# Reordering the opening of a fused depthwise-conv and feed-forward kernel: conv by token halves, other splits of loads, and output slots ahead of the second group

## The chip, the cores and the metric

The kernel runs on one core of one Trainium2 chip. The metric is device time in microseconds (us); the time before is the median of three runs. The engines are named as in the profile: PE is TensorE, DVE is VectorE, ACT is ScalarE, POOL is GpSimd, SP is SyncE. The last two mostly issue DMAs here.

## The reference

```
def attn(x, weight):                     # x (8, 4096, 192) f32, weight (8 heads, 7 taps)
    w = softmax(weight, axis=-1)         # with + 1e-9 in the denominator
    x_pad = zeros of 6 tokens in front of each sequence, then x
    out[b, s, h, g] = sum_k w[h, k] * x_pad[b, s + k, h, g]      # 24 channels a head

def moe(x, w_in, w_out):                 # x (32768, 192), w_in (192, 2048), w_out (2048, 192)
    h = x @ w_in
    g = maximum(0.01 * h, h)
    return g @ w_out

reference = moe(attn(x, weight).reshape(32768, 192), w_in, w_out)
```

A causal depthwise convolution of 7 taps, a matrix product up to 2048 features, a leaky relu, and a matrix product back to 192.

## The kernel before

**Layout.** Channels stand on partitions: three chunks `c` of 64 channels, and two batches (`e` = 0, 1) on the two partition halves. `xt` holds the transposed input, `yt` the result of the conv, `g` the relu's output. A *block* is 512 tokens of a pair of batches; there are 32. Blocks 0 and 1 are cut into halves of 256 tokens, so the list `groups` has four groups of 256 (0 to 3) and then 30 of 512.

**Stages of a group.** (1) The conv makes `yt` from `xt`. On DVE it is `conv_jobs`: for each chunk, one multiplication (L222) and six multiply-adds (L228) with the taps in `wk`. On PE it is `pe_conv_jobs` (L259): a tap is a diagonal matrix `diag[c]`, in a high and a low part, so that a chunk takes 2 parts x 7 taps x 2 batches = 28 matmuls, accumulated in a PSUM tile `acc` and then scaled by `rsum` into `yt` (`evac`; straight at L271, crossed between the partition halves at L276). Straight and crossed jobs run side by side on the array. (2) `mm1` (L507) makes one unit `u`: 12 matmuls of 256 columns into one of two `ph` buffers in PSUM, then a Prelu on ACT (L515) writes `g` and frees the buffer. A group of 256 tokens has eight units (two feature chunks of 128 each). (3) `mm2` multiplies by `w_out`. For groups 0 to 3 it runs in row slots (`mm2_row_slot`, L525): a slot is two matmuls, for the two row halves of one feature chunk `fc` and a pair `p` of output tiles; round 0 and round 1 of a pair swap the halves, and between the rounds stands a *seal*, a small ACT instruction (or an output copy on ACT) that the first slot of the next round waits for. Later groups use the transposed form at L588, which this change leaves alone.

**The opening.** Only groups 0 and 1 have a conv on PE. Group 0: chunk 0 by its two parts in two accumulators (`hi`, and `low` through ACT, joined by DVE at L465), then chunks 1 and 2. Group 1: chunk 1 on DVE, chunks 0 and 2 on PE in three pieces, which `CUTS` puts behind the units 1, 3 and 5 of group 0. From group 2 on the conv is all DVE's, in the order `SKEW`, issued one group ahead.

Input: `x_half` 0 is loaded by SP and transposed on PE. `x_rows` 1 and 2 (groups 1 and 2) are loaded by POOL, transposed on PE (L167, `transpose_first`) into the PSUM tile `ptr`, and copied into `xt` by `evac_first` (L195). `x_half` 3 and all later blocks are loaded by POOL's DMAs and transposed by DMAs that SP issues. `w_in[0]` and `w_in[1]` are loaded by POOL; copies on DVE (`spread_up` L326, `spread_down` L322) put the rows also on the other partition half. `near` and `far` are the halves of the 1024 columns of one `w_in`.

**What sets the order.** The schedule is by hand: each engine runs its instructions in the order of the program text. POOL issues, in this order: `w_in` 0 in three DMAs with `x_rows` 1 between, `w_in` 1 in two, `x_rows` 2, `w_out` in two, then computes `wk` (L445, L446), then issues `x_half` 3 and block 2. `plan`, `quota` and `between` say how many mm2 row slots stand between and behind mm1's units in each step of two units; the slots of group i belong to the tiles of group i - 1.

PSUM: `ptr`, `acc` and `po` tiles share one ring of four buffers, so a new one waits until the oldest has been read.

Of the kernel before, what the change touches and what calls it, by code (L numbers as in the profile page):

```python
# [10 lines left out]
FP32 = mybir.dt.float32  # L11
BF16 = mybir.dt.bfloat16
# [3 lines left out]
def kernel(  # L16
# [33 lines left out]
    for k in range(K):  # L50
        SKEW += [(2, k), next(pair)]
    SKEW += [(1, 5), (0, 6), (1, 6)]
    CUTS = {1: (0, 6), 3: (6, 11), 5: (11, 14)}
    GB = 32
    NR = D // (2 * GB)

# [79 lines left out]

    def load_first(q):
        rows = x[0:2, q * HT : (q + 1) * HT, :].rearrange("e (s p) d -> p e s d", s=HS)
        if q == 0:
            x_nat[q] = stage_pool.tile([128, 2, HS, D], FP32, name="x_nat")  # L140
            for s in range(HS):
                nc.sync.dma_start(out=x_nat[q][:, :, s], in_=rows[:, :, s])
        elif q in x_rows:
            for e in range(2):
                nc.gpsimd.dma_start(out=x_rows[q][:, e], in_=rows[:, e])  # L145
        else:
            for c in range(NCH):
                for e in range(2):
                    nc.gpsimd.dma_start(  # L149
                        out=x_half[q][:, c, :, e, :],  # L150
                        in_=rows[:, e, :, c * CH : (c + 1) * CH],
                    )
# [9 lines left out]
    def transpose_first(q, mid=None):  # L162
        if q:
            t = psum_o.tile([128, HS, NCH, 128], BF16, name="ptr", tag="po")
            for s, c in product(range(HS), range(NCH)):
                for e in range(2):
                    nc.tensor.transpose(  # L167
                        out=t[e * CH : (e + 1) * CH, s, c, :],
                        in_=x_rows[q][:, e, s, c * CH : (c + 1) * CH],
                        identity=ident,  # L170
                    )
            ptr[q] = [t[:, s] for s in range(HS)]
            return
        ts = [
            psum_o.tile([128, NCH, 128], FP32, name=f"ptr{s}", tag="po") for s in range(HS)
        ]
        for s, t in enumerate(ts):
            if s and mid is not None:
                mid()
            for c in range(NCH):  # L180
                nc.tensor.matmul(
                    out=t[:, c, :],
                    lhsT=x_half[q][:, c, s, :, :].rearrange("p e k -> p (e k)"),
                    rhs=ident,
                    start=True,
                    stop=True,
                )
        ptr[q] = ts

    def evac_first(q, *copies):  # L190
        dst = xt[0][:, :, HALO + q * HT : HALO + (q + 1) * HT]
        dst = dst.rearrange("p c (s k) -> p s c k", s=HS)
        for s, t in enumerate(ptr.pop(q)):
            for cs in (slice(0, 1), slice(1, NCH)) if q == 0 and s else (slice(0, NCH),):
                copies[s](out=dst[:, s, cs], in_=t[:, cs])  # L195

    def transpose_half(q):
# [123 lines left out]
    def spread_down(n, copy=nc.vector.tensor_copy, cols=slice(0, WF)):  # L321
        copy(out=w_in[n][0:CH, 1, cols], in_=w_in[n][CH:128, 0, cols])  # L322
# [16 lines left out]
    load_w_in(0, 128, near)  # L339
    load_first(1)  # L340
    load_w_in(0, 128, far)
    for rows in (0, 128):
        load_w_in(1, rows)
    load_first(2)


    w_out = const_pool.tile([128, NFC, D], BF16)
    for h in range(2):
        cs = slice(h * NFC // (2 * RUN), (h + 1) * NFC // (2 * RUN))
        nc.gpsimd.dma_start(  # L350
            out=w_out.rearrange("p (c i) d -> p c i d", i=RUN)[:, cs],
            in_=moe_w_out.rearrange("(c p i) d -> p c i d", p=128, i=RUN)[:, cs],
        )


    wa = psum_h.tile([128, 2, ST], FP32, name="warm", tag="ph")
# [87 lines left out]
    wk = const_pool.tile([128, NCH, K], FP32, name="wk")  # L444
    nc.gpsimd.tensor_add(wk, taps[:, :, 0, 0:K, 0], wml[:, :, 0:K])  # L445
    nc.gpsimd.tensor_mul(wk, wk, rsum.to_broadcast([128, NCH, K]))  # L446
    load_first(3)
    load_x(2)
    diag_wide(1, 1)
    diag_wide(2, 1)  # L450
    spread_up(0, slice(0, 1), near)
    spread_down(0, cols=near)

    def act_scale(out, in_, scale):
        nc.scalar.activation(
            out=out, in_=in_, func=mybir.ActivationFunctionType.Copy, scale=scale
        )

    hi = acc_tile()
    low = const_pool.tile([128, HT], FP32, name="low")  # L460
    pe_hi, _ = pe_conv_jobs(groups[0], 0, parts=(0,), accs=[hi] * 2)
    pe_lo, evac_lo = pe_conv_jobs(groups[0], 0, cross=True, parts=(1,))
    run(pe_hi, pe_lo)
    evac_lo(act_scale, act_scale, out=low)
    nc.vector.scalar_tensor_tensor(  # L465
        out=y_of(groups[0], 0), in0=hi[:, :HT], scalar=rsum[:, 0, :], in1=low,
        op0=mybir.AluOpType.mult, op1=mybir.AluOpType.add,
    )
    spread_up(0, slice(2, 3), near)
    pe_1, evac_1 = pe_conv_jobs(groups[0], 1)  # L470
    pe_2, evac_2 = pe_conv_jobs(groups[0], 2, cross=True, accs=[acc_tile(), wps[:, 0]])
# [1 line left out]
    evac_1(act_scale)  # L473
    evac_2(nc.vector.tensor_scalar_mul, act_scale)
    spread_up(0, slice(0, 1), far)
    spread_down(0, nc.scalar.copy, far)


    g, po, acc2, osb, seal = {}, {}, {}, {}, None
# [8 lines left out]
    def mm1(grp, u, M):  # L488
# [9 lines left out]
        if wide:  # L498
            order = [(i, c) for c in chunks for i in range(nf)]
        for i, c in order:  # L500
            if wide and (i, c) == (0, 2):
                transpose_first(1)
            f = nf * u + i
            for e in range(2):
# [17 lines left out]
    def mm2_one(rt, m, fc, start, stop):  # L522
# [7 lines left out]
            stop=stop,  # L530
        )

    def mm2_row_slot(q):

        p, fc = divmod(q, 2 * NFC)
        rnd, fc = divmod(fc, NFC)
        pair = (2 * p, 2 * p + 1)
        first, last = fc == 0, fc == NFC - 1  # L540
# [112 lines left out]
        NSW - 1: [8, 8, 16, 16],  # L653
        NSW: [16, 8, 8, 16, 8, 8, 16, 16],
    }
    between = {(1, 0): (3, 5)}
    for i, js in ((NSW - 2, (2, 3)), (NSW - 1, (1, 2)), (NSW, (2, 3, 5, 6))):
        between.update({(i, j): (0, 4) for j in js})
    slot = 0
# [10 lines left out]
    for i, grp in enumerate(groups):  # L670
        blk, t0, T = grp
        steps = T // 64
        if t0 == 0:
            g[blk] = g_pool.tile([128, NFC, 2, ST], BF16, name="g", tag="g")
        quota = plan.get(i, [16] * 4 if T == HT else [5, 5, 6, 5, 5, 6, 8, 8])

        if i == 0:
            ahead = []
# [3 lines left out]
        for j in range(steps):  # L682
            early = between.get((i, j), (0, 0))
            for u in range(2 * j, 2 * j + 2):
                mm2_slots(i, early[u % 2])
                mm1(grp, u, 128 if i <= NSW else CH)
                if i == 0 and u == 0:
                    evac_first(1, nc.vector.tensor_copy, nc.vector.tensor_copy)
                    spread_up(0, slice(2, 3), far)
                    conv_1 = conv_jobs(groups[1], (1,))  # L690
                    run([conv_1[:3]])
                    spread_down(1)
                    spread_up(1, slice(0, 1), near)
                    spread_up(1, slice(2, 3))
                    run([conv_1[3:5]])
                    spread_up(1, slice(0, 1), far)
                    run([conv_1[5:]])
                    pe_0, evac_0 = pe_conv_jobs(groups[1], 0)
                    pe_2, evac_2 = pe_conv_jobs(groups[1], 2, cross=True)
                if i == 0 and u in CUTS:  # L700
                    cut = slice(*CUTS[u])
                    run(pe_0[cut], pe_2[cut])
                if i == 0 and u == 5:
                    evac_0(nc.vector.tensor_scalar_mul)
                    evac_2(nc.vector.tensor_scalar_mul, nc.vector.tensor_scalar_mul)
                if i == 0 and u == 6:
                    transpose_first(2)
                    evac_first(2, nc.vector.tensor_copy, nc.vector.tensor_copy)
            jobs = ahead[per * j : per * (j + 1)]
            if T == ST:  # L710

# [56 lines left out]
```

## Time and profile before

| what | value |
|---|---|
| median of the runs | 680.82 us (680.67 to 681.41, 3 runs) |
| span of the profiled execution | 679.2 us |
| PE busy | 674.9 us (99%) |
| ACT busy | 517.6 us (76%), 496.6 of it the Prelu L515 |
| DVE busy | 481.2 us (71%), 380.1 of it the conv L228 |
| POOL busy | 147.4 us (22%) |
| one Prelu (128x1024) | 1.02 us |
| first mm1 matmul | 8.09 us after the span's start |
| landing of `w_in[1]` | 12.19 and 12.77 us |
| landing of `x_rows` 2 | 13.28 and 13.81 us |
| landing of `w_out` | 15.73 and 17.59 us |

The span runs from the first to the last recorded instruction. A chain of waits lists what ended last, followed back from the end; its pieces are start, length, engine, tile and line, and how many instructions. In a timeline or a group line, `out<-in partitions x elements` says what an instruction reads and writes, and the bracket behind it the idle time of its engine just before and what ended that. Start-to-start spacings of single instructions are a little shorter than the durations, because an engine overlaps one's end with the next one's start.

### The profile page before, as it was taken

The numbers are of one execution on the slowest core, as the hardware profiler recorded it, in microseconds if no ns is written. First come the engines' busy times: TensorE is split into PE (matmuls) and PEld (weight loads), VectorE is DVE, ScalarE is ACT, GpSimd is POOL, SyncE is SP. The second block draws the span as 40 slices with busy tenths as digits, with TensorE's granted clock in tenths as the row PEclk, the third lists the DMA queues.
The fourth block names the chain that finished last, engine by engine and source line by source line (L and its number), as shares of the span: only waits on it lengthen the run. The fifth ranks groups of instructions, "written<-read, shape, count | busy, mean of one in ns | idle before, by whom it ended". The sixth has DMA issues, their size and how long they took to land.

```text
span 679.2 us, 27092 instructions
## 1 busy us (share of the span) xinstructions
PE 674.9 (99%) x12442; PEld 446.3 (66%) x12442; DVE 481.2 (71%) x816; ACT 517.6 (76%) x601; POOL 147.4 (22%) x208
## 2 busy tenths in 40 slices
PE   9999999999999999999999999999999999999998
PEld 6997666666666666666666666666666666666667
DVE  7989477866768766778667687667786676876612
ACT  7899877777787777777777777778777777777781
POOL 8455221122211222211222112222022220000000
PEclk9999999999999999999999999999999999999999
DMA  9999755655737656556556566567365573321123
GB/s 149 99 119 104 52 85 83 84 64 67 96 74 93 76 54 86 84 85 86 66 63 92 80 92 78 56 83 94 73 87 69 60 96 71 72 56 33 34 49 94
DMA packets 213970, 53.27 MB, mean 78 GB/s; under 512 B 209312, under 2 KB 213536, under 8 KB 213856
## 3 DMA queue, kind: packets, MB, share of 16 engines
q0 software_dynamic: 98832, 13.97, 30.3%
q1 hardware_dynamic: 115008, 37.57, 28.0%
q8 instruction: 97, 1.59, 0.9%
q14 instruction: 17, 0.14, 0.1%
q10 hardware_dynamic: 16, 0.00, 0.0%
HBM read 28.31 MB, written 25.17 MB: 79 GB/s over the span
## 4 chain that ended last, share of the span: by engine, by line
PE 98%; DVE 1%; ACT 0%; issue 0%; ACTq 0%
PE ph L507 49%; PE acc L588 44%; PE po L525 5%; PE acc L259 0%; DVE diag L420 0%; PE ptr L167 0%; ACT L366 0%; ACTq L288 0%; DVE w_in L322 0%; DVE yt L465 0%; DVE o_sb L638 0%; DVE x_half L155 0%; ACT w L372 0%; DVE w_in L326 0%; ACT junk L366 0%
## 5 line engine op out<-in xcount | busy, mean ns | idle before, releaser
L515 ACT ACTIVATE g<-ph 128x1024 bf16<-128x1024 f32 x512 | 496.6, 1021 | 139.8 <-PE ph L507 139.6
L228 DVE SCALAR_TENSOR_TENSOR yt<-xt,wk,yt 128x512 bf16<-128x512 bf16 (+1 forms) x582 | 380.1, 715 | 0.2
L507 PE MATMUL ph<-yt,w_in 64*64 64x512 bf16 (+2 forms) x6048 | 377.5, 369 | 0.3 <-DVE yt L465 0.3
L588 PE MATMUL acc<-g,w_out 64*64 64x512 bf16 x5568 | 339.9, 376 | 0.0
L507 PEld LDWEIGHTS <-w_in 64*64 64x64 bf16 (+1 forms) x6048 | 229.7, 131 | 103.4 <-issue 1.1
L588 PEld LDWEIGHTS <-w_out 64*64 64x64 bf16 x5568 | 178.2, 118 | 118.8
L96 POOL DMA_DIRECT2D x_bf<-in_x_dram x180 | 133.9, 774 | 407.6 <-DMA xt<-x_bf 405.6
L610 DVE STREAM_TRANSPOSE o_t<-acc 128x512 f32<-128x512 f32 x87 | 72.9, 875 | 182.2 <-PE acc L588 182.2
L525 PE MATMUL po<-w_out,g 64*128 64x192 bf16 (+1 forms) x640 | 36.8, 243 | 0.0
L525 PEld LDWEIGHTS <-g 64*128 64x128 bf16 (+1 forms) x640 | 32.6, 95 | 3.2 <-issue 0.4
L222 DVE TENSOR_SCALAR yt<-xt,wk 128x512 bf16<-128x512 bf16 (+1 forms) x97 | 28.8, 320 | 2.4 <-DMA xt<-x_bf 2.4
L598 ACT COPY junk<-junk 128x1 f32<-128x1 f32 x58 | 11.1, 191 | 4.1
L638 DVE COPY o_sb<-po 128x192 f32<-128x192 f32 x8 | 2.8, 356 | 6.8 <-PE po L525 3.9
L638 ACT COPY o_sb<-po 128x192 f32<-128x192 f32 x16 | 5.1, 323 | 0.3
L259 PE MATMUL acc<-xt,diag 64*64 64x256 bf16 x126 | 4.7, 272 | 0.1
L149 POOL DMA_DIRECT2D x_half<-in_x_dram x6 | 4.3, 732 | 0.9 <-DMA w_in<-in_moe_w_in_dram 0.9
L259 PEld LDWEIGHTS <-diag 64*64 64x64 bf16 x140 | 3.7, 106 | 1.0 <-issue 0.4
L360 PE MATMUL warm<-const-bfloat16-1.0 128*128 128x512 bf16 (+2 forms) x8 | 3.3, 577 | 0.8 <-PEq L752 0.8
L145 POOL DMA_DIRECT2D x_rows<-in_x_dram x4 | 2.9, 746 | 0.0
L316 POOL DMA_DIRECT2D w_in<-in_moe_w_in_dram x5 | 2.9, 593 | 0.0
L360 PEld LDWEIGHTS <-const-bfloat16-1.0 128*128 128x128 bf16 x10 | 1.2, 128 | 2.2 <-issue 2.2
L326 DVE COPY w_in<-w_in 64x512 bf16<-64x512 bf16 (+1 forms) x7 | 2.3, 337 | 0.2
(52 smaller groups left out, 25.9 us busy)
## 6 DMA issues: line engine op xcount, KB each, us to landing
out_dram<-o_t SPq DMA_DIRECT2D x112, 192.0 KB, 4.7
x_bf<-in_x_dram POOLq DMA_DIRECT2D x180, 64.0 KB, 3.1
out_dram<-o_sb SPq DMA_DIRECT2D x8, 192.0 KB, 2.8
xt<-x_bf SPq DMA_TRANSPOSE x90, 3.2
w_out<-in_moe_w_out_dram POOLq DMA_DIRECT2D x2, 384.0 KB, 8.3
out_dram<-o_t SPq DMA_DIRECT2D x8, 96.0 KB, 2.4
out_dram<-o_sb SPq DMA_DIRECT2D x8, 96.0 KB, 1.7
w_in<-in_moe_w_in_dram POOLq DMA_DIRECT2D x2, 256.0 KB, 5.5
```

Of the source, the lines that this page charges most:

```text
L96: ins = nc.gpsimd.dma_start(out=t[:, c, :, e, :], in_=src[2 * rp + e, :, :, c * CH : (c + 1) * CH],)
L222: lambda s=src, d=dst, c=c: nc.vector.tensor_scalar_mul(d, s, wk[:, c, 0:1])
L228: lambda s=src, d=dst, c=c, k=k: nc.vector.scalar_tensor_tensor(out=d, in0=s, scalar=wk[:, c, k : k + 1], in1=d, op0=mybir.AluOpType.mult, ...
L259: lambda k=k, p=p, a=a, ps=ps, to=to, acc=accs[e]: nc.tensor.matmul(out=acc[to, :T], lhsT=diag[c][ps, p, k, :], rhs=xt[0][ps, c, a : a + T ...
L360: nc.tensor.matmul(out=to[:, 0:cols], lhsT=ones[:, 0:128], rhs=ones[:, 0:cols], start=True, stop=True,)
L507: nc.tensor.matmul(out=ph[m : m + M, e, i * T : (i + 1) * T], lhsT=w_in_of(f, e, c, m, m + M), rhs=y[ps, c, t0 : t0 + T], start=(c == chun ...
L515: act = nc.scalar.activation(out=g[blk][:, nf * u : nf * (u + 1), :, t0 : t0 + T], in_=ph.rearrange("p e (i t) -> p i e t", i=nf), func=my ...
L525: return nc.tensor.matmul(out=po[m], lhsT=g[b][ps, fc, e, s * 128 : (s + 1) * 128], rhs=w_out[ps, fc, :], start=start, stop=stop,)
L588: ins = nc.tensor.matmul(out=acc2[gi, r][e * CH : (e + 1) * CH, 0:T], lhsT=w_out_of(ps, fc, r), rhs=g[b][ps, fc, e, t0 : t0 + T], start=fi ...
L598: seal = nc.scalar.copy(out=junk, in_=junk)
L610: nc.vector.transpose(out=osb[gi, 0][:, 0 : T // GB, :, r], in_=acc2.pop((gi, r))[:, 0:T].rearrange("p (j k) -> p j k", k=GB),)
L638: ins = copy(out=o_sb[:, n % 2, :], in_=po.pop(n))
```

## The change

1. Group 0's chunk 0: no parts in two accumulators any more. The conv is done by two halves of 128 tokens, both parts each (`pe_conv_halves`), and ACT alone writes `yt`. The join at L465 is gone; the spread of `w_in[0]`'s far half downwards goes from ACT to DVE, and two spreads move behind the conv in the text.
2. Group 1's conv: `CUTS` is gone. Chunk 0 alone runs on PE, by token halves, in one piece behind unit 4; chunks 1 and 2 are 14 jobs on DVE, the last four behind the evacuation of chunk 0.
3. `w_in[1]` is loaded in column halves, four DMAs for two, and spread in six copies.
4. `x_rows` holds tokens in pairs: partition p has tokens 2p and 2p + 1. The evacuation reads `ptr` with the token parity innermost, chunks 1 and 2 first and chunk 0 then. For `x_rows` 2 it goes from DVE to ACT.
5. `w_out`'s two DMAs are issued behind `wk`.
6. `x_rows` 1 is transposed after 4 matmuls of unit 0 instead of 8.
7. Row slots: the first 64 are taken in another order (`row_slots`), 16 of them run ahead of group 1's unit 0 and 4 between units 0 and 1, and the rest of group 1's are spread between the units.

```diff
-    CUTS = {1: (0, 6), 3: (6, 11), 5: (11, 14)}
...
     def load_first(q):
         rows = x[0:2, q * HT : (q + 1) * HT, :].rearrange("e (s p) d -> p e s d", s=HS)
+        if q in x_rows:
+            rows = x[0:2, q * HT : (q + 1) * HT, :].rearrange("e (p s) d -> p e s d", s=HS)
...
-            ptr[q] = [t[:, s] for s in range(HS)]
+            ptr[q] = t
             return
...
     def evac_first(q, *copies):
         dst = xt[0][:, :, HALO + q * HT : HALO + (q + 1) * HT]
+        if q:
+            dst = dst.rearrange("p c (k s) -> p c k s", s=HS)
+            t = ptr.pop(q).rearrange("p s c k -> p c k s")
+            for copy, cs in zip(copies, (slice(1, NCH), slice(0, 1))):
+                copy(out=dst[:, cs], in_=t[:, cs])
+            return
         dst = dst.rearrange("p c (s k) -> p s c k", s=HS)
         for s, t in enumerate(ptr.pop(q)):
-            for cs in (slice(0, 1), slice(1, NCH)) if q == 0 and s else (slice(0, NCH),):
+            for cs in (slice(0, 1), slice(1, NCH)) if s else (slice(0, NCH),):
                 copies[s](out=dst[:, s, cs], in_=t[:, cs])
...
-    for rows in (0, 128):
-        load_w_in(1, rows)
+    for cols in (near, far):
+        for rows in (0, 128):
+            load_w_in(1, rows, cols)
     load_first(2)
-    w_out = const_pool.tile([128, NFC, D], BF16)
-    for h in range(2):
...
     nc.gpsimd.tensor_mul(wk, wk, rsum.to_broadcast([128, NCH, K]))
+    w_out = const_pool.tile([128, NFC, D], BF16)
+    for h in range(2):
...
     load_first(3)
     load_x(2)
     diag_wide(1, 1)
     diag_wide(2, 1)
-    spread_up(0, slice(0, 1), near)
-    spread_down(0, cols=near)
...
-    hi = acc_tile()
-    low = const_pool.tile([128, HT], FP32, name="low")
-    pe_hi, _ = pe_conv_jobs(groups[0], 0, parts=(0,), accs=[hi] * 2)
-    pe_lo, evac_lo = pe_conv_jobs(groups[0], 0, cross=True, parts=(1,))
-    run(pe_hi, pe_lo)
-    evac_lo(act_scale, act_scale, out=low)
-    nc.vector.scalar_tensor_tensor(
-        out=y_of(groups[0], 0), in0=hi[:, :HT], scalar=rsum[:, 0, :], in1=low,
-        op0=mybir.AluOpType.mult, op1=mybir.AluOpType.add,
-    )
+    def pe_conv_halves(grp, c):
+        blk, t0, T = grp
+        return (
+            pe_conv_jobs((blk, t0, T // 2), c),
+            pe_conv_jobs((blk, t0 + T // 2, T // 2), c, cross=True),
+        )
+
+    (pe_a, evac_a), (pe_b, evac_b) = pe_conv_halves(groups[0], 0)
+    run(pe_a, pe_b)
+    evac_a(act_scale)
+    evac_b(act_scale, act_scale)
+    spread_up(0, slice(0, 1), near)
+    spread_down(0, cols=near)
     spread_up(0, slice(2, 3), near)
...
-    spread_down(0, nc.scalar.copy, far)
+    spread_down(0, cols=far)
...
-            if wide and (i, c) == (0, 2):
+            if wide and (i, c) == (0, 1):
                 transpose_first(1)
...
+    row_slots = list(range(2 * NSW * 2 * NFC))
+    first_half = NFC // 2
+    row_slots[: 4 * NFC] = [
+        p * 2 * NFC + rnd * NFC + fc
+        for p, rnd, fcs in (
+            (0, 0, range(first_half)),
+            (1, 0, range(first_half)),
+            (0, 0, range(first_half, NFC)),
+            (0, 1, range(NFC)),
+            (1, 0, range(first_half, NFC)),
+            (1, 1, range(NFC)),
+        )
+        for fc in fcs
+    ]
...
-        p, fc = divmod(q, 2 * NFC)
+        p, fc = divmod(row_slots[q], 2 * NFC)
...
-    between = {(1, 0): (3, 5)}
+    between = {(1, 0): (16, 4), (1, 1): (0, 8), (1, 2): (0, 8), (1, 3): (0, 8)}
...
-        quota = plan.get(i, [16] * 4 if T == HT else [5, 5, 6, 5, 5, 6, 8, 8])
+        quota = plan.get(i, [24, 16, 16, 8] if T == HT else [5, 5, 6, 5, 5, 6, 8, 8])
...
                     spread_up(0, slice(2, 3), far)
-                    conv_1 = conv_jobs(groups[1], (1,))
-                    run([conv_1[:3]])
-                    spread_down(1)
+                    conv_1 = conv_jobs(groups[1], (1, 2))
+                    run([conv_1[:4]])
+                    spread_down(1, cols=near)
                     spread_up(1, slice(0, 1), near)
-                    spread_up(1, slice(2, 3))
-                    run([conv_1[3:5]])
+                    spread_up(1, slice(2, 3), near)
+                    run([conv_1[4:6]])
+                    spread_down(1, cols=far)
                     spread_up(1, slice(0, 1), far)
-                    run([conv_1[5:]])
-                    pe_0, evac_0 = pe_conv_jobs(groups[1], 0)
-                    pe_2, evac_2 = pe_conv_jobs(groups[1], 2, cross=True)
-                if i == 0 and u in CUTS:
-                    cut = slice(*CUTS[u])
-                    run(pe_0[cut], pe_2[cut])
-                if i == 0 and u == 5:
-                    evac_0(nc.vector.tensor_scalar_mul)
-                    evac_2(nc.vector.tensor_scalar_mul, nc.vector.tensor_scalar_mul)
+                    spread_up(1, slice(2, 3), far)
+                    run([conv_1[6:10]])
+                if i == 0 and u == 4:
+                    (pe_a, evac_a), (pe_b, evac_b) = pe_conv_halves(groups[1], 0)
+                    run(pe_a, pe_b)
+                    evac_a(nc.vector.tensor_scalar_mul)
+                    evac_b(nc.vector.tensor_scalar_mul, nc.vector.tensor_scalar_mul)
+                    run([conv_1[10:]])
                 if i == 0 and u == 6:
                     transpose_first(2)
-                    evac_first(2, nc.vector.tensor_copy, nc.vector.tensor_copy)
+                    evac_first(2, nc.scalar.copy, nc.scalar.copy)
```

## The prediction

> **What bounds the kernel now.** I read the page first: the busy rows and the shares of the chain that ended last.
>
> ```profile
> PE 674.9 (99%) x12442; PEld 446.3 (66%) x12442; DVE 481.2 (71%) x816; ACT 517.6 (76%) x601; POOL 147.4 (22%) x208
> ...
> PE 98%; DVE 1%; ACT 0%; issue 0%; ACTq 0%
> ```
>
> TensorE (PE) holds the chain for 98% of the span. The span is 679.2 us; the median of the runs is 680.82, so 1.6 us lie around the span. PE has no slack after 8 us: a microsecond that it waits anywhere arrives at the end, and one that it saves is kept unless something else then makes it wait. All edits act before about 32 us, so next I read the chain of waits there (start, length, what).
>
> ```profile
> 8.09 0.63 PE ph L507 x8
> ...
> 10.18 0.78 PE acc L259 x24
> 10.96 1.44 PE ph L507 x24
> 12.40 0.67 PE acc L259 x20
> 13.07 1.68 PE ph L507 x24
> 14.75 0.45 PE acc L259 x12
> ...
> 17.29 0.25 PE po L525 x6
> ...
> 19.26 0.66 PE po L525 x16
> 19.92 1.31 PE ph L507 x24
> ```
>
> Group 1's conv is three pieces (0.78, 0.67, 0.45, sum 1.90). A stretch of 24 mm1 matmuls costs 1.31 at 19.92, between mm2 pieces, and 1.44 and 1.68 after a conv piece. So mm1 (0.65 per u) and mm2 (16 in 0.66) alternate for nothing, while each conv piece adds 0.1 to 0.2 on either side. Then the timeline of VectorE (DVE):
>
> ```profile
> 7.56 0.48 DVE L465 SCALAR_TENSOR_TENSOR yt<-acc,rsum,low 128x256 bf16<-128x256 f32 x1
> ...
> 12.21 0.42 DVE L322 COPY w_in<-w_in 64x1024 bf16<-64x1024 bf16 x1 [0.61 <-DMA w_in<-in_moe_w_in_dram]
> ...
> 15.72 0.48 DVE L271 TENSOR_SCALAR yt<-acc,rsum 128x256 bf16<-128x256 f32 x1
> 16.23 1.00 DVE L276 TENSOR_SCALAR yt<-acc,rsum 64x256 bf16<-64x256 f32 x2
> 17.27 0.62 DVE L195 COPY xt<-ptr 128x384 bf16<-128x384 bf16 x2
> 17.92 0.72 DVE L222 TENSOR_SCALAR yt<-xt,wk 128x256 bf16<-128x256 bf16 x2
> ```
>
> From 6.67 to 17.92 DVE stands still once, for the 0.61 shown. At 17.92 it begins group 2's conv, and it has no pause until 46.16, where block 2's conv ends; PE starts block 2 at 46.04. So DVE is the second full engine of this stretch.
>
> **DVE's list, the term that decides.** I redo 6.67 to 17.92 by start-to-start spacings.
> - Removed: L465, 0.52. The two copies at 17.27 go to ACT: 0.66 (17.92 - 17.27). The 0.61 wait for w_in: w_in[1] now comes in four pieces, and the first two, half of the 384 KB, should be there before DVE reaches them (about 11.6); I take the whole 0.61, bounds 0 to 0.61.
> - Shorter: the three evacuations at 15.72 to 17.27 (1.54) have 128 columns instead of 256. Half would be 0.77, unchanged 1.54; nothing between is shown, I take 1.14, so -0.40.
> - Added: seven more conv jobs. Today's seven cost 3.30 without the wait, because each waits for its forerunner in the same chunk (spacing 0.52). With chunks 1 and 2 alternating, the spacing is that of group 2's conv at 17.92: 0.20 for the two L222, 0.396 for L228. 2 x 0.20 + 12 x 0.396 = 5.15, so +1.85.
> - spread_down of w_in[0]'s far half comes from ACT: rows give 0.22 (half of the 64x1024 copy's 0.44) to 0.58 (the 64x512 one at 6.97); +0.33. w_in[1]'s spreads become six copies of 64x512 (0.21 to 0.39 each), 1.80 for 1.56: +0.24.
> - evac_first(1) reads PSUM with a stride. No row has that. Low bound: today's 0.66 unchanged. High bound: 768 columns at the pace of the f32 evacuation (0.51 per 256), 1.53. Source and bytes are as today, only the step differs, so nearer the low end: +0.30.
>
> Sum: -0.52 - 0.66 - 0.61 - 0.40 + 1.85 + 0.33 + 0.24 + 0.30 = +0.53. The last job of group 1's conv ends at 18.45, not at some 16.
>
> [...]
>
> **The new wait.** evac_first(2) now runs on ACT. Its first copy writes chunks 1 and 2 of xt in one instruction whose address range (first chunk's start to last chunk's end) encloses the columns of chunk 2 that group 1's conv reads. On DVE, program order covered that; on ACT it is a wait for the last conv job (chunk 2, tap 6). Queued behind it on ACT: the second copy and the Prelu of u7 (17.33 today). Behind these stand PE's ninth mm2 slot, whose bank the copies empty, and DVE's first group 2 job, which reads what they write.
>
> ACT's cost: 128x256 casts from PSUM take 0.378, 128x128 ones 0.267, so 512 columns 0.60 and 256 columns 0.38: 0.98 (bounds: 0.65, the two rows as they stand; 1.42, three of the 128x256 f32 evacuations of 0.474). With 0.05 for a handover (matmul end to Prelu is 0.04): copies 18.50 to 19.48, slot 8 and group 2's conv at 19.53.
>
> **PE from there.** Slots 8 to 15 (16 matmuls) 0.66, group 1's u0 0.65, slots 16 to 19 0.33: 21.17. The old kernel has, at 19.92, 32 mm2 matmuls, u0 and u1 done; the same work as mine (40 and u0) stands at 19.92 - 0.65 + 0.33 = 19.60. So **+1.57**.
> Then the new interleaving, with the Prelu at 1.02 (0.92 back to back):
> - The seal of pair 0 is queued on ACT behind u1's Prelu (21.86 to 22.88), ends at 23.07; only u2's mm1 (to 22.81) covers it: +0.31. Today 24 matmuls do.
> - Pair 1's seal, an output copy of 0.32 behind u4's Prelu, covered by u5 alone: +0.14.
> - u7 and group 2's u0 and u1 stand in a row. Three units need three Prelus through two ph buffers: the third waits for u7's Prelu (about 29.9 to 30.9) when PE is ready at 30.5: +0.49. Today two units stand between 32-matmul blocks.
> From group 2's u1 on the programs are alike. Sum 1.57 + 0.31 + 0.14 + 0.49 = **+2.51**: span 681.7, time 683.3.
>
> **What PE saves lies ahead of the wait and is lost in it.** Start: mm1 need no longer wait for L465 at 8.04, only for the conv's last matmul (7.75): -0.3 to -0.45. Group 1's conv has 14 rounds of four 64x128 matmuls. Low bound: the 128-column transposes, 12 in 0.46, 0.077 a pair side by side, and 0.055 as half of a 64x256 round; high bound 0.109 as today's whole round. 0.77 to 1.53 for 1.90; I take 0.9, -1.0; two conv pieces fewer, about -0.5. All that makes PE reach slot 8 by about 17, where it stands until 19.53; a dearer round changes nothing unless it passes 2 us. Transposing after 4 matmuls instead of 8 only lets DVE's copies start sooner, and DVE is not free before 9.0. With five units in a row (u0 to u4), Prelus at 0.92 set the pace; hidden too.
>
> [...]
>
> **Queues.** POOL issues two more w_in DMAs (0.54 to 0.69 each), so all behind them goes out 1.1 to 1.35 later: x_rows 2 (lands 13.81, needed before 18), w_out (15.73 and 17.59, needed about 18.8 and 20.8), x_half 3 (18.98; its chunk transposes feed DVE only behind group 2's conv). All have cover; it runs out if w_in's far half, needed at 13.2 and landing at 12.77 today, passes the delay on. wk goes ahead of w_out's 1.48, so no later than today's 10.09. Nothing changes on SP's queue. x_rows' longer runs can only help.
>
> **DVE at block 2.** Its conv starts 1.61 late and ends at 47.77; PE, 2.51 late, comes at 48.55. Hidden; without PE's delay it would show.
>
> **Rivals.**
> 1. PE's savings carry through (0.06). Start 0.4, conv 1.0, borders 0.5: -1.9, and 680.8 becomes 678.9. For: 98% of the chain. Against: block 2's first matmul on chunk 1 is at 46.26 and DVE ends it at 46.16, a cover of 0.1 in which PE can gain nothing unless DVE's list shrinks too, by 1.8 for this time, and it grows by 0.53.
> 2. The copies do not wait for the last conv job, or cost almost nothing (0.16). Then DVE's list alone decides, at block 2: +0.53 - 0.10 = +0.43, PE's own stalls (0.94) against 1.9 saved: **681.3**, not distinguishable from before. It decides if the copies start before about 17.
> 3. A late transfer (0.16): w_in's far half lands 1.2 later, 14.0 for 13.2, and DVE waits 0.8 ahead of the same chain: 684.1.
>
> **Numbers.** Forecast 0.62: 683.3. With the low prices (strided copy +0, ACT 0.65, half of the later stalls) it is 1.1 less, 682.2; with the high ones (evacuations +0.4, strided copy +0.5 more) 684.2. For 8 in 10 I reach down to rival 2: 681.2 to 684.4. What a measurement can tell here is 0.2%, 1.36 us: faster 0.06 (rival 1), same 0.16 (rival 2), slower 0.78 (forecast and rival 3).
>
> **What the profile will show.** Right: ACT idle before the L195-type copies until about 18.5, released by DVE's L228; u7's Prelu near 19.4 instead of 17.33; a PE gap of 2 us inside the first mm2 slots; group 2's conv near 19.5; PE waits for ACT after group 1's u2 and before group 2's u1. First mm1 near 7.7. Wrong: the copies running by 17, or DVE idle between 13 and 18 for w_in (rival 3), or conv jobs spaced at 0.5.

## The result, and the profile after

| | before | changed |
|---|---|---|
| median | 681.03 us (4 runs, 680.67 to 681.41) | 685.42 us (4 runs: 685.19, 685.39, 685.46, 686.44) |
| span of the profiled execution | 679.2 us | 684.7 us (the run of 686.44) |

The changed kernel is slower: ratio 1.0069, 95% interval 1.0055 to 1.0083, or +4.4 us. The forecast had the direction and most of the mechanism, but +2.5; the time lies above the range. The profiled execution is the slowest of the four, 0.98 us above the next, and that difference is part of the story.

The busy row of PE on the page of the changed kernel:

```profile
PE 677.1 (99%) x12470; PEld 449.7 (66%) x12470; DVE 483.6 (71%) x823; ACT 517.9 (76%) x603; POOL 147.6 (22%) x210
```

PE is still busy for 99%, and busy 2.2 us longer although its 28 extra matmuls are small ones. Busy time does not tell why: a matmul at a lower clock counts as busy too (1.30 of the 1.30 us from 21.40, at a clock of 0.50, in the stretches below). The chain of waits (start, length, what) does:

```profile
17.90 1.68 DVE yt L235 x4
...
19.66 0.87 ACT xt L197 x2
...
20.58 0.84 PE po L531 x15
21.41 1.28 PE ph L513 x12
22.69 0.64 PE po L531 x8
23.33 1.29 PE ph L513 x12
...
25.57 0.19 ACT junk L581
...
32.79 1.03 ACT g L521
33.86 0.85 PE ph L513 x12
```

Before, the chain was PE's from 8.09 us on. Now it is DVE's until 19.6, then ACT's two copies, then PE. ACT's timeline has the wait in its brackets (idle before, and what ended it):

```profile
19.66 0.86 ACT L197 COPY xt<-ptr 128x512 bf16<-128x512 bf16 x2 [2.31 <-DVE yt L235]
20.41 1.04 ACT L521 ACTIVATE g<-ph 128x1024 bf16<-128x1024 f32 x1
```

ACT's copies wait 2.31 us for DVE's last conv job, and the Prelu of u7, 17.33 before, follows at 20.41. DVE's timeline shows why that job is late:

```profile
8.89 1.02 DVE L197 COPY xt<-ptr 128x512 bf16<-128x512 bf16 x2
...
10.27 0.58 DVE L229 TENSOR_SCALAR yt<-xt,wk 128x256 bf16<-128x256 bf16 x2
10.82 0.88 DVE L235 SCALAR_TENSOR_TENSOR yt<-xt,wk,yt 128x256 bf16<-128x256 bf16 x2
11.74 0.54 DVE L329 COPY w_in<-w_in 64x512 bf16<-64x512 bf16 x1
12.29 0.71 DVE L333 COPY w_in<-w_in 64x512 bf16<-64x512 bf16 x2
13.04 0.88 DVE L235 SCALAR_TENSOR_TENSOR yt<-xt,wk,yt 128x256 bf16<-128x256 bf16 x2
13.95 0.49 DVE L329 COPY w_in<-w_in 64x512 bf16<-64x512 bf16 x1
14.45 0.71 DVE L333 COPY w_in<-w_in 64x512 bf16<-64x512 bf16 x2
15.19 1.67 DVE L235 SCALAR_TENSOR_TENSOR yt<-xt,wk,yt 128x256 bf16<-128x256 bf16 x4
16.78 0.34 DVE L278 TENSOR_SCALAR yt<-acc,rsum 128x128 bf16<-128x128 f32 x1
17.16 0.71 DVE L283 TENSOR_SCALAR yt<-acc,rsum 64x128 bf16<-64x128 f32 x2
17.90 1.67 DVE L235 SCALAR_TENSOR_TENSOR yt<-xt,wk,yt 128x256 bf16<-128x256 bf16 x4
20.56 0.57 DVE L229 TENSOR_SCALAR yt<-xt,wk 128x256 bf16<-128x256 bf16 x2 [0.98 <-ACT xt L197]
```

The wait of 0.61 for w_in is gone, but w_in[1]'s six spreads fill 11.74 to 13.04 and 13.95 to 15.19, 2.54 us where three took 1.56. The conv ends at 19.58, and then DVE itself waits 0.98 for ACT before group 2. Last, the view of chosen stretches (stretch, its length, busy time of PE, PEld, DVE, ACT and POOL with instructions, the granted clock, DMA share, GB/s):

```profile
15.40:18.10 2.70, 2.69 (x53) 2.21 (x50) 2.62 (x8) 1.94 (x2) 0.81 (x2) 1.00 1.58 141
...
21.40:22.70 1.30, 1.30 (x18) 1.30 (x15) 1.30 (x5) 0.05 (x1) 0.36 (x1) 0.50 2.67 144
22.70:23.35 0.65, 0.65 (x12) 0.65 (x9) 0.65 (x3) 0.62 (x1) 0.00 (x0) 0.50 1.40 33
23.35:24.60 1.25, 1.25 (x16) 1.25 (x14) 1.25 (x5) 0.40 (x1) 0.00 (x0) 0.50 1.33 116
24.60:25.80 1.20, 1.08 (x21) 0.81 (x15) 1.20 (x4) 1.15 (x3) 0.00 (x0) 0.98 0.64 110
```

After PE's stand of 2.4 us the granted clock is 0.50 until 24.6. That is why units 0 and 1 of group 1 take 1.28 us in the chain instead of 0.65. No term of the forecast had this.

### The profile page after: what moved, and what is told of

The parts are those of the page before. It is cut to its first block, busy times and chain, and to the rows that moved or that the text cites. A ratio compares the mean times of both kernels' runs of the same rounds, so it can differ in the third digit from the quotient of the medians.

```text
span 684.7 us, 27160 instructions
## 1 busy us (share of the span) xinstructions
PE 677.1 (99%) x12470; PEld 449.7 (66%) x12470; DVE 483.6 (71%) x823; ACT 517.9 (76%) x603; POOL 147.6 (22%) x210
## 4 chain that ended last, share of the span: by engine, by line
PE 97%; DVE 2%; ACT 0%; issue 0%; ACTq 0%
PE ph L513 48%; PE acc L609 44%; PE po L531 5%; DVE yt L235 1%; PE warm L359 0%; PE acc L266 0%; DVE w_in L333 0%; ACT g L521 0%; DVE w_in L329 0%; DVE yt L283 0%; DVE xt L197 0%; ACT xt L197 0%; DVE yt L229 0%; PE ptr L182 0%; DVE o_sb L659 0%
## 5 line engine op out<-in xcount | busy, mean ns | idle before, releaser
L235 DVE SCALAR_TENSOR_TENSOR yt<-xt,wk,yt 128x512 bf16<-128x512 bf16 (+1 forms) x588 | 383.0, 719 | 0.1
L513 PEld LDWEIGHTS <-w_in 64*64 64x64 bf16 (+1 forms) x6048 | 232.3, 131 | 104.1 <-DVE w_in L333 1.5
L531 PE MATMUL po<-w_out,g 64*128 64x192 bf16 (+1 forms) x640 | 39.0, 246 | 2.6 <-ACT xt L197 2.4
L531 PEld LDWEIGHTS <-g 64*128 64x128 bf16 (+1 forms) x640 | 34.7, 96 | 5.6 <-issue 3.0
L266 PE MATMUL acc<-xt,diag 64*64 64x128 bf16 (+1 forms) x154 | 3.7, 232 | 0.0
L333 DVE COPY w_in<-w_in 64x512 bf16<-64x512 bf16 x8 | 2.7, 353 | 0.1
```

The source lines that it names most:

```text
L235: lambda s=src, d=dst, c=c, k=k: nc.vector.scalar_tensor_tensor(out=d, in0=s, scalar=wk[:, c, k : k + 1], in1=d, op0=mybir.AluOpType.mult, ...
L266: lambda k=k, p=p, a=a, ps=ps, to=to, acc=accs[e]: nc.tensor.matmul(out=acc[to, :T], lhsT=diag[c][ps, p, k, :], rhs=xt[0][ps, c, a : a + T ...
L513: nc.tensor.matmul(out=ph[m : m + M, e, i * T : (i + 1) * T], lhsT=w_in_of(f, e, c, m, m + M), rhs=y[ps, c, t0 : t0 + T], start=(c == chun ...
L531: return nc.tensor.matmul(out=po[m], lhsT=g[b][ps, fc, e, s * 128 : (s + 1) * 128], rhs=w_out[ps, fc, :], start=start, stop=stop,)
```

## The experiments

Medians stand beside the runs of the kernel before that ran with them (681.0 to 681.2); intervals are of the ratio. "Less" and "more" are in us.

### The wait of ACT's copies for the last conv job: a1, a2

```diff
-            for copy, cs in zip(copies, (slice(1, NCH), slice(0, 1))):
+            parts = (slice(1, NCH), slice(0, 1)) if q == 1 else (slice(1, 2), slice(2, 3), slice(0, 1))
+            for copy, cs in zip(copies, parts):
...
-                    evac_first(2, nc.scalar.copy, nc.scalar.copy)
+                    evac_first(2, *[nc.scalar.copy] * 3)
```

> The changed kernel, but ACT copies x_rows 2 out of PSUM in three copies of one chunk each, so that no copy's address range encloses another chunk. Theory (the wait of ACT's copies for the last conv job is the largest part of the loss): the copies run near 17 us instead of 19.7, u7's Prelu near 18.4 instead of 20.4, PE passes slot 8 near 18.2 and stands only for the conv's end (19.6) ahead of group 1's unit 0; some 1.6 to 2 us less, about 683.6. Rival 1 (DVE's list alone decides, wherever the copies are): 1.0 us less at most, since group 2's conv starts at 19.6 instead of 20.6: 684.4. Rival 2 (the order of the slots costs the time): unchanged, 685.4.

Measured 682.83 (1.0014 to 1.0036), 2.6 less than the changed kernel. The timelines of ACT and of PE:

```profile
17.66 0.93 ACT L198 COPY xt<-ptr 128x256 bf16<-128x256 bf16 x3
18.44 1.08 ACT L522 ACTIVATE g<-ph 128x1024 bf16<-128x1024 f32 x1
```

```profile
18.64 0.82 PE L532 MATMUL po<-w_out,g 64*128 64x192 bf16 x15 [0.18 <-ACT xt L198]
19.23 1.21 PE L514 MATMUL ph<-yt,w_in 64*128 64x256 bf16 x12
```

Three copies of one chunk need no wait and run straight behind u6's Prelu. PE waits 0.18 at slot 8 instead of 2.41, and group 1's unit 0 stretches to 1.21 because its later chunks are not ready before 19.8. So the wait (2.31 us on ACT in the changed kernel, none here) was not for data: the same bytes are written, only the address range that one instruction covers is different. No other single edit takes off more. The DVE-list rival is out as the sole cause (684.4), and so is the slots' order.

The other way to be rid of ACT's wait, copies by DVE:

```diff
-                    evac_first(2, nc.scalar.copy, nc.scalar.copy)
+                    evac_first(2, nc.vector.tensor_copy, nc.vector.tensor_copy)
```

> The changed kernel, but DVE does the two copies of x_rows 2 again, behind its conv jobs. Theory (the place of the copies behind the conv's last job costs, on either engine): copies on DVE from 19.6 to 20.6, slot 8 and group 2's conv near 20.6 as now, u7's Prelu back at 17.4: 684.8 to 685.4. Rival (what costs is that the Prelu of u7 is queued behind ACT's copies): 683.5 or less, as the wait moves off ACT.

Measured 685.48 (1.0054 to 1.0079): nothing gained. u7's Prelu follows u6's without a wait again, and PE's slot 8 still waits 2.59 us, now for DVE. What costs is the copies' place behind the conv, not ACT's queue.

### DVE's list: a4, c1

```diff
-                    conv_1 = conv_jobs(groups[1], (1, 2))
+                    conv_1 = conv_jobs(groups[1], (1,))
...
-                    (pe_a, evac_a), (pe_b, evac_b) = pe_conv_halves(groups[1], 0)
-                    run(pe_a, pe_b)
+                    pe_0, evac_0 = pe_conv_jobs(groups[1], 0)
+                    pe_2, evac_2 = pe_conv_jobs(groups[1], 2, cross=True)
+                    run(pe_0, pe_2)
...
```

> The changed kernel, but PE makes chunk 0 and chunk 2 of group 1 (56 matmuls of 256 columns in one piece behind unit 4), DVE only chunk 1. Theory (DVE's list, longer by the second chunk, sets when everything behind it starts): DVE's list is 2 us shorter, the copies run near 17.8 to 18.6, PE pays 0.65 more for conv: 682.5 to 683.5, and TensorE shows no clock below 1. Rival (the loss lies in ACT's copies or in the slots' order, not in DVE's list): 685 or more.

Measured 682.96 (1.0019 to 1.004), 2.5 less. DVE is done with group 1 at 17.3, ACT's copies run from 17.66 without a wait, and PE has no stand at slot 8. PE pays 1.66 us for the conv's one piece. The late conv and the copy that waits for its end are two conditions of the same stand, so the 2.6 of a1 and the 2.5 of a4 are not to be added.

```diff
-    for cols in (near, far):
-        for rows in (0, 128):
-            load_w_in(1, rows, cols)
+    for rows in (0, 128):
+        load_w_in(1, rows)
...
-                    spread_down(1, cols=near)
+                    spread_down(1)
                     spread_up(1, slice(0, 1), near)
-                    spread_up(1, slice(2, 3), near)
+                    spread_up(1, slice(2, 3))
...
-                    spread_down(1, cols=far)
                     spread_up(1, slice(0, 1), far)
-                    spread_up(1, slice(2, 3), far)
```

> The changed kernel with edit 3 undone: w_in 1 in two DMAs and spread in three copies of up to 1024 columns, as before. Theory (DVE's list sets the wait, and six spreads cost it 2.54 us where three cost 1.56): the copies of ACT start up to 1.0 us sooner if w_in's landing does not hold DVE up again, 684.2 to 684.6; 0.6 less than that gain if DVE waits for the landing as before. Rival (the halves are worth it, since DVE stood 0.61 for w_in): 685.4 or more.

Measured 684.29 (1.0037 to 1.0063), 1.1 less in the medians, though the two intervals overlap. Its profile has slot 8 at 20.14, 0.70 before the third repeat below (d2), which also has the full clock; so the halves of w_in[1] cost some 0.7 to 1.1. DVE did not have to wait for the whole w_in here either, because its list reaches the spread at 12.37, not at 11.6 as in the kernel before.

### The order of the slots: b2, a3

```diff
-    between = {(1, 0): (3, 5)}
+    between = {(1, 0): (16, 4), (1, 1): (0, 8), (1, 2): (0, 8), (1, 3): (0, 8)}
...
-        quota = plan.get(i, [16] * 4 if T == HT else [5, 5, 6, 5, 5, 6, 8, 8])
+        quota = plan.get(i, [24, 16, 16, 8] if T == HT else [5, 5, 6, 5, 5, 6, 8, 8])
```

and `row_slots` as in the change, on the kernel before.

> The kernel before, with edit 7 alone: the new order and places of the row slots, no wait on DVE or ACT put in front of them. Theory (the order pays at both seals and at three units in a row, 0.3 + 0.1 + 0.5): 0.9 us more than before, 682.1, with the third unit of the row waiting 0.45 for a Prelu. Rival (the order costs only where the waits of the other edits have already delayed ACT): no difference, 681.2.

Measured 682.41 (1.0013 to 1.003), 1.3 more. Its chain of waits:

```profile
18.41 0.67 PE ph L507 x12
...
19.11 2.02 ACT g L515 x2
...
21.14 0.20 ACT junk L575
...
21.38 0.83 PE po L525 x16
...
28.36 1.03 ACT g L515
...
29.44 0.85 PE ph L507 x12
```

The seal (junk) stands behind two Prelus and PE waits for it; later group 2's unit 1 waits for a Prelu at 28.36. These are two of the three places that the forecast named, here without any other edit.

a3 is the reverse: the changed kernel with `between`, `quota` and `row_slots` as before.

> The changed kernel with the row slots in the old order and places (3 slots, unit 0, 5 slots, unit 1, 16 slots behind every two units). Theory (the new interleaving costs 0.3 + 0.1 + 0.5 us at the seals and at three units in a row, but its 16 slots ahead hide 1.3 us of the wait for DVE): about 0.5 us less or the same, 684.9 to 685.4. Rival 1 (interleaving is a main part of the loss): 684.4 or less. Rival 2 (the slots ahead are what softens the wait): 686 or more.

Measured 684.99 (1.0043 to 1.0068), 0.4 less, with the clock at half in four of five runs; the fifth, at full clock, took 683.68, where the changed kernel's executions at full clock took 684.25 to 685.46. At half clock it is 684.93 to 685.71 against 686.44 and 686.65. So like against like the old order is 0.6 to 1.8 us less, and the medians differ by only 0.4 because the clock fell in more of a3's runs. That the slots ahead give back a part of the order's price isn't shown.

### The clock: c3

```diff
+                if i == 1 and u == 0:
+                    mm2_slots(i, 8)
+                    ph_next[blk, t0, 0] = psum_h.tile([128, 2, ST], FP32, name="ph", tag="ph")
+                    warm(20, HT, ph_next[blk, t0, 0][:, 0])
+                    mm2_slots(i, early[0] - 8)
```

The 20 extra matmuls write a buffer that unit 0 then overwrites.

> The changed kernel with 20 matmuls of 256 columns that nobody reads, on PE behind the eighth row slot, where PE stands for the copies of ACT. Theory (PE's clock falls to half after a stand of 2.4 us, in some executions and not in others, and costs 1.0 to 1.3 us there): the clock stays at 1.00 in the stretch after the wait, the units behind it take 0.65 instead of 1.28, no execution is above 685.8, the median 684.8 to 685.4. Rival 1 (the slow units have another cause, such as contention for yt or w_in): they stay at 1.28, and the median at 685.4 with some runs above 686. Rival 2 (the wait ends sooner when PE works): below 684.5.

Measured 685.36 (1.0048 to 1.0073), runs from 684.28 to 685.54. PE's timeline, and a row of the same stretch as above:

```profile
18.81 2.41 PE L359 MATMUL ph<-const-bfloat16-1.0 128*128 128x256 bf16 x20
21.16 0.92 PE L535 MATMUL po<-w_out,g 64*128 64x192 bf16 x16
21.85 0.88 PE L517 MATMUL ph<-yt,w_in 64*128 64x256 bf16 x12
```

```profile
21.40:22.70 1.30, 1.30 (x33) 1.30 (x30) 1.30 (x6) 0.74 (x1) 0.56 (x1) 1.00 1.29 22
```

The view reads a clock of 1.00. This trace holds no clock record of its own, so the pace is the evidence: the slots behind the wait keep it (33 matmuls in the stretch where the changed kernel had 18), and no run is above 685.6. That agrees with the clock as the cause of the slow units, which the rows at 0.50 show. It is not proof that the work prevents the fall: at 2 falls in 7 executions of the changed kernel (with those of d2), five runs without one come by chance about one time in five. The last section has more on it. The median is unchanged, because most runs of the changed kernel had the full clock anyway. This profiled execution began 1.1 us late (an input landed at 5.08 us instead of 3.9), so its starts aren't compared with the others.

### The changed kernel three more times: d2

No edit. The question was where executions at full clock spend their 4 us.

> The changed kernel once more. Theory 1 (an execution at full clock is the one whose input lands late, by about 1.1 us, and so has the other terms the same): clock 1.00, first diagonal 1.1 us later than 4.5 us, wait for the copies as long, 685.4. Theory 2 (the clock falls or not by chance of its window): first diagonal at 4.5 in all, slot 8 near 20.6, and the units behind it at 0.65 or at 1.28; then 684.8 and 686.4.

> The changed kernel once more, as d2_again_1: full clock and a late input at 685.4, or 686.4 with the clock at half behind the wait and the input at its usual time.

> The changed kernel once more, as d2_again_1: full clock and a late input at 685.4, or 686.4 with the clock at half behind the wait and the input at its usual time.

Measured 686.65, 684.25 and 685.11. The first has the clock at 0.50 behind the wait, the others 1.00, and the input landed at 3.9 us in all three, so theory 1 falls. Part of PE's timeline of the second and of the third:

```profile
19.97 0.82 PE L531 MATMUL po<-w_out,g 64*128 64x192 bf16 x15 [2.33 <-ACT xt L197]
20.56 0.88 PE L513 MATMUL ph<-yt,w_in 64*128 64x256 bf16 x12
```

```profile
20.84 0.82 PE L531 MATMUL po<-w_out,g 64*128 64x192 bf16 x15 [2.41 <-ACT xt L197]
21.43 0.88 PE L513 MATMUL ph<-yt,w_in 64*128 64x256 bf16 x12
```

The wait is in both, and it ends at 19.97 or at 20.84. In the second, DVE's spreads were short:

```profile
11.68 0.29 DVE L329 COPY w_in<-w_in 64x512 bf16<-64x512 bf16 x1
...
13.51 0.32 DVE L329 COPY w_in<-w_in 64x512 bf16<-64x512 bf16 x1
```

In the third, DVE stood 0.66 us for a conv of PE that ran late in the first microseconds. So there are two chances in this kernel's time: when DVE's list ends, and whether the clock falls (2 of 7 executions).

### Parts alone on the kernel before: b1, d1, b3

b1 is edit 1 alone: chunk 0 by token halves, all on ACT, no L465, the far spread on DVE.

```diff
-    run(pe_hi, pe_lo)
-    evac_lo(act_scale, act_scale, out=low)
-    nc.vector.scalar_tensor_tensor(
...
+    run(pe_a, pe_b)
+    evac_a(act_scale)
+    evac_b(act_scale, act_scale)
...
-    spread_down(0, nc.scalar.copy, far)
+    spread_down(0, cols=far)
```

> The kernel before, with edit 1 of the change alone: group 0's chunk 0 by token halves, evacuated by ACT, no join on DVE, the far spread of w_in 0 on DVE. Theory (PE's gain at the start is real, and what it is worth is set by DVE at block 2): mm1 starts 0.4 us sooner, DVE's list is 0.2 shorter; 0.2 to 0.4 us less than before, 680.8 to 681.0. Rival (PE has the chain from 8 us on, so all of the start's 0.45 arrives): 680.7. If the halves cost anything (weight loads at 128 columns): 681.2 or more.

Measured 681.15 (0.9994 to 1.0012): no difference. In its chain mm1's second chunk waits until 8.41 for ACT's evacuation of conv chunk 1, so the early start of the first four matmuls is lost at once. d1 covers that wait with the transposes (and keeps the far spread on ACT):

```diff
-            if wide and (i, c) == (0, 2):
+            if wide and (i, c) == (0, 1):
                 transpose_first(1)
```

> The kernel before with edits 1 and 6 only (group 0's chunk 0 by token halves, far spread left on ACT; x_rows 1 transposed after 4 matmuls), conv of group 1 in three pieces as before. Theory (the start's gain is real, since PE has the chain, and DVE's list is 0.5 shorter, so block 2 can follow): 0.3 to 0.4 us less than before, 680.6 to 680.8. Rival (the gain is lost at the Prelus' pace as in the two-piece kernel): 681.0 or more.

Measured 681.45 (0.9995 to 1.0013): no difference either, the rival's side. Its profiled execution had a slow conv in the first microseconds (mm1 at 8.33), which hides what the edit could give; whether a gain of 0.2 us exists is open.

b3 is the pairing of tokens alone, both evacuations on DVE.

```diff
+        if q in x_rows:
+            rows = x[0:2, q * HT : (q + 1) * HT, :].rearrange("e (p s) d -> p e s d", s=HS)
...
+            for copy, cs in zip(copies, (slice(1, NCH), slice(0, 1))):
+                copy(out=dst[:, cs], in_=t[:, cs])
+            return
```

> The kernel before, with edit 4's pairing of tokens alone, both evacuations on DVE. Theory (DVE's delay arrives at block 2, where its cover is 0.1): each evacuation with a stride takes 0.4 us longer, group 2's conv starts 0.8 us late, block 2's first units wait 0.7 for chunk 1: 681.9. Rival 1 (DVE's delay is absorbed, since PE has the chain): 681.2. Rival 2 (the longer runs of the loads let everything start sooner): below 681.

Measured 681.55 (0.9998 to 1.0016), about 0.5 more, at the edge of what can be told. The chain, which ended in PE alone before, now holds DVE up to block 2:

```profile
39.86 6.64 DVE yt L236 x10
46.50 0.04 issue
46.54 1.27 PE ph L515 x10
```

Each evacuation takes 1.02 instead of 0.62. DVE's delay does arrive at block 2 when PE is not late itself.

### Repairs: b4, c2, c4

b4 is a4 with the old order of slots.

> The changed kernel with chunk 2 of group 1 back on PE and the old order of the slots. Theory (the three parts of the loss are DVE's list, the wait and clock behind it, and the order of slots): 0.9 us less than with the new order, 682.0, the rest being five units in a row, with PE waiting for Prelus. Rival (the order is worth nothing by itself): 683.0 as with the new order.

Measured 682.10 (1.0007 to 1.0024): 0.86 less than a4, near the order's price. It is still 1.0 above the kernel before; its PE waits for Prelus three times in the five units in a row and behind them (0.46 at 10.52, 0.20 at 12.49, 0.42 at 19.49), as its expectation has it, but no run takes these waits away. c2 puts three repairs into the changed kernel: a1's copies, c1's whole w_in, the old slots.

> The changed kernel with three parts mended at once: copies of x_rows 2 chunk by chunk on ACT, w_in 1 in two DMAs and three copies, the old order of slots. Theory (the terms add): 682.8 with the chunk copies alone, less some 0.8 for the slots' order and up to 0.6 for DVE's list: 681.4 to 682.0. Rival (they overlap, each hides the next): 682.5 or more.

Measured 682.55 (1.0013 to 1.0031), only 0.3 less than a1 alone (0.1 when each is set against the runs of the kernel before beside it). The terms do not add: without the slots ahead PE reaches group 1's unit 0 at once and stands there for the conv's last job, which DVE still ends at 19.14. The second chunk on DVE is then part of what is left; b4, which has it on PE, is 0.45 lower. c4 went the other way, from the kernel before:

```diff
-    CUTS = {1: (0, 6), 3: (6, 11), 5: (11, 14)}
+    CUTS = {1: (0, 7), 4: (7, 14)}
...
-                if i == 0 and u == 5:
+                if i == 0 and u == 4:
```

with d1's edits; the last line moves the conv's evacuation.

> The kernel before with what the runs left over as gains: group 0's chunk 0 by token halves (far spread on ACT as before), x_rows 1 transposed after 4 matmuls instead of 8, so that the transposes stand where unit 0 waits for chunk 1, and group 1's conv in two pieces (behind units 1 and 4) instead of three. Theory: 0.15 at the start and 0.25 for one conv piece fewer, DVE's list 0.5 shorter: 680.6 to 680.8, for 681.1. Rival (the Prelus' pace holds PE at the longer run of units): 681.1 or more.

Measured 681.51 (1.0002 to 1.002): 0.5 more, the rival's side. u7 starts at 16.85 instead of 16.44; with the conv in two pieces the units crowd, and PE waits 0.46 us for a Prelu at 12.62. No kernel here is faster than the one before.

## Why the prediction was right in direction and too small

The forecast's sum against three executions of the changed kernel (starts in us, differences in brackets; spans against 679.2):

| term | forecast | profiled (686.44) | second repeat (684.25) | third repeat (685.11) |
|---|---|---|---|---|
| slot 8 starts | 19.53 | 20.58 (+1.05) | 19.97 (+0.44) | 20.84 (+1.31) |
| clock at half behind it | none | +1.67 | 0 | 0 |
| start set against end | none | +0.17 | +0.17 | +0.17 |
| forecast's sum with these | +2.51 | +5.40 | +3.12 | +3.99 |
| span measured | | +5.5 | +3.3 | +4.2 |

The 1.67 is the excess of the two units and 16 matmuls at 21.17 to 24.80 over their 1.96 at full clock (3.63 - 1.96).

1. **The step that failed is the sum of DVE's list**, "+0.53. The last job of group 1's conv ends at 18.45". It ended at 19.58 in the profiled execution, at 18.97 in the second repeat and at 19.83 in the third. Mis-sized in the profiled one were w_in[1]'s spreads (1.80 booked, 2.54 measured; c1's three copies take 1.47), the 14 conv jobs (5.15 booked, 5.64: the job ahead of a copy is waited out, 0.51 instead of 0.40, at two places; the second multiplication takes 0.35 instead of 0.20; and the last job counts with its whole 0.48) and the strided evacuation (0.96 booked, 1.05). The rest of the list came some 0.2 sooner than booked. The evacuations by halves (1.14 booked, 1.12) and the wait of 0.61 that vanishes were right.
2. **A term was missing: the clock.** The forecast let PE stand 2.5 us and priced only the stand. The stretches show 0.50 behind it, and in c3, where PE stays at work, no run has it. It cost 1.67 in the profiled execution. Whole runs that have it differ by less, 1.0 to 1.25 (686.44 against 685.19 to 685.46), since the others can lose time elsewhere, as the third repeat does. It is not in the median.
3. **A slip of bookkeeping**: slot 8's time is a start, while 19.60 came from the chain, whose pieces stand 0.17 later than the starts in the timeline (19.26 against 19.09 for the same matmuls).
4. **The new wait** was right in place and cause: released by DVE's L235 (the lines of the conv's L228), with u7's Prelu behind it and slot 8 and group 2's conv behind the copies. The copies took 0.86 for 0.98 booked. a1 shows the wait to be one of address range only.
5. **The order of slots** was right in its places and priced too low. By the matmuls' starts PE loses 0.35, 0.18 and 0.62 in the profiled execution, 1.15 for the 0.94 booked (0.31, 0.14, 0.49). b2 has the order alone: 0.52, 0.18 and 0.62 there make 1.32, and its median is 1.34 above the kernel before. The 0.2 that is missing is about what the table leaves open (0.1 to 0.2).
6. **PE's savings lost in the wait** was right: mm1 at 7.63 for 8.09, the conv's piece 0.92 for 0.9. b1 and d1, without the wait, show no gain from the start either; by their intervals a gain above 0.4 us is out, a smaller one stays open.
7. **DVE's delay at block 2, hidden behind PE's**, was right: in the profiled execution DVE ends block 2's conv at 49.45 and PE begins block 2 at 51.60. b3 uncovers the delay.
8. **The rivals.** PE's savings carrying through did not happen. The second, copies that need not wait, is a1: 682.8, not the 681.3 given, since unit 0 still needs the conv's end and the order still costs. The third did not happen: w_in's last quarter landed at 11.69, before its use at 13.95. x_rows' loads with the longer runs took a median of 4.3 us from issue to landing for 5.2; the DMAs issued around them had changed too.

The range was too narrow for a reason that can be named: its upper end added up dearer evacuations, but no dearer spreads and nothing for a clock of 0.50 behind a long stand.

## What to carry to other kernels

An edit that takes work off the full engine must be priced on the engine that receives it, with every instruction that it splits: here the split copies and the second chunk cost DVE more than PE got (5.64 us of conv jobs for 3.30 and 2.54 of spreads for 1.56, against 0.92 of conv on PE for 1.90). When a copy moves to another engine, look at the whole address range that one instruction encloses, since program order no longer covers a false overlap; one copy per chunk was worth 2.6 us. And a stand of PE can have a second price, the clock after it: 0.50 in two of seven executions of the changed kernel, at 1.67 us in the profiled one; it is best avoided.

## What the runs showed of the hardware that was not expected

**The clock after a stand.** Behind a stand of about 2.4 us the clock was 0.50 for 3.4 us (21.2 to 24.6) in some executions of the changed kernel and not in others, with the same stand (2.41 us in the first and the third repeat). In all four profiles with a fall the trace's clock record begins at 4.0 to 4.2 us and the fall comes 17.07 us later, five times the 3.41 us that the clock then stays low. Laid out in steps of 3.41 us from where each record begins, the step with the least work of PE around the stand is:

| execution | step (us) | PE busy in it | clock behind it |
|---|---|---|---|
| changed, profiled | 17.83 to 21.25 | 1.01 of 3.42 | 0.50 |
| changed, first repeat | 17.69 to 21.10 | 1.00 of 3.41 | 0.50 |
| a2 | 17.79 to 21.20 | 0.87 of 3.41 | 0.50 |
| a3 | 17.65 to 21.06 | 1.50 of 3.41 | 0.50 |
| changed, second repeat | 18.42 to 21.83 | 1.86 of 3.41 | 1.00 |
| changed, third repeat | 16.31 to 19.72 | 2.11 of 3.41 | 1.00 |
| c1 | 16.52 to 19.93 | 2.01 of 3.41 | 1.00 |

So in these seven the clock fell behind steps in which PE was busy for 26 to 44%, and stayed behind those with 55 to 62%; a3 had no stand above 1.04 us, but two in one step. By this layout the chance lies in how the stand falls on the steps: in the second and third repeat it is spread over two. That the steps run on in the executions without a fall is inferred. One more point agrees with it: in the profile before, the clock record begins at 4.08 us and the clock goes to 0.50 at 679.92, behind the last instruction, 198.0 steps of 3.413 us later. Why the clock falls, no run shows.

**DVE copies that end with POOL's DMA issues.** The same 64x512 copy took from 0.29 to 0.59 us. The end of each slow one follows the end of a DMA issue on POOL by the same time:

| kernel, copy's start to end | POOL's issue ends | difference |
|---|---|---|
| before, 6.974 to 7.524 | 7.411 | 0.113 |
| changed, 11.736 to 12.280 | 12.172 | 0.108 |
| changed, 12.503 to 13.004 | 12.890 | 0.114 |
| changed, 13.948 to 14.438 | 14.325 | 0.113 |

In the second repeat the copies at 11.68 and 13.51 fell early in an issue or at its end and took 0.29 and 0.32. Over all 18 profiles, 37 of these 64x512 copies of w_in took 0.40 us or more, and every one of them ended 0.09 to 0.12 us after the end of an issue on POOL. So a DMA issue on POOL seems to hold such a copy of DVE until it ends. That is inferred from the times; no run took the issues away. In the changed kernel's profile four of w_in[1]'s six spreads end so, each some 0.2 us longer than the others (0.49 to 0.54 against 0.29), about what the six took above their price.

**The first microseconds differ between executions.** Two matmuls of 128 rows (512 and 192 columns) on PE at about 4.7 us took 0.46 together in the profile before and 0.79 in the third repeat. The view of stretches reads a clock of 1.00 in both, but the trace's clock record begins at 4.08 us in the first and at 6.07 in the third repeat. In the eleven profiles whose record begins by 4.76 the pair took 0.46 or 0.47, in the five where it begins at 5.57 or later 0.79 or 0.80; so the view's 1.00 ahead of the record is not a measurement. That the clock was low there is an inference from the 0.79 against 0.46. With the slower pair mm1's start comes up to 0.5 us later (8.16 for 7.63 in the changed kernel), more than the change could gain there.
